# W2 sums on POOL, later low parts and spread stores in a linear-attention and two-MoE kernel

## The chip, the cores and the metric

The kernel runs on one core of one Trainium2 chip. The metric is the device time of one execution in microseconds (us), lower is better. Engines: TensorE (PE, with its weight loads PEld), VectorE (DVE), ScalarE (ACT), GpSimd (POOL) and SyncE (SP), which here only issues DMA transfers. Each engine works through its own list in order; semaphores order the lists among each other.

## The reference

Three stages in float32. Linear attention with a root-mean-square norm gives x of N = 2304 rows and D = 512 columns. A dense mixture of E = 8 experts (F = 1024) follows, whose gates come from 8 Sinkhorn rounds; then a second mixture in which each row goes to one expert, chosen by the cosine to an embedding.

```python
kv = einsum('bhsd,bhse->bhde', k, v); out = einsum('bhsd,bhde->bhse', q, kv)
x = out / sqrt(mean(out * out) + 1e-6) * g_norm
P = exp(x @ w_gate - max)
for _ in range(8):
    P /= P.sum(1, keepdims=True) + 1e-9
    P /= P.sum(0, keepdims=True) + 1e-9
    P *= N / E
x2 = sum over e of P[:, e:e+1] * (maximum(x @ w1[e], 0) @ w2[e])
expert = argmax(cosine(x2, expert_emb) / tau); gate = softmax at expert
out[rows of e] = gate * (maximum(x2 @ w1b[e], 0) @ w2b[e])
```

## The kernel before

**Number format.** Every float32 operand is split in two: a high part (`wh`, made on ScalarE, line 163) and a low part, the difference (`wl`, line 168 on POOL in two halves of 512 columns, line 170 on VectorE in one piece). A product is three matmuls: high x high, high x low, low x high.

**Steps.** The dense mixture is done in 3 blocks of 768 rows. Block b and expert e make step s = 8 b + e, 24 steps. Each has an up phase (7 products `n` = 0 to 6 with W1, a fast matrix scheme that needs sums and differences of the quarters of W1 and x; 4 positions `i` each, 28 positions, 6 matmuls a position) and a down phase with W2. In block 0 (steps 0 to 7) the down phase is plain: 4 parts `m` of 6 positions. In steps 8 to 22 it uses the fast scheme as well (7 products of 3 positions), and so needs differences of the quarters of W2. Step 23 is followed by the second mixture.

In the profiled execution steps 1 to 9 begin their up phases at 151.71, 222.43, 293.39, 357.47, 429.06, 497.20, 566.51, 631.83 and 696.25 us; step 15 at 1052.38, step 16 at 1112.26, step 17 at 1180.34. The fast steps between last about 59.3 us each. The down phases of steps 2 to 7 begin at 256.84, 324.79, 394.67, 462.78, 531.96 and 598.55.

**Weights ahead.** `ahead(g)` (line 936, called in the second position of each up product and the third of each down part) prepares part g + 3 with `prep`: the high part on ScalarE, the low part on POOL for n in 3, 5, 6, 8, 9 and on VectorE else, and for n = 2 and 3 two differences of quarters on POOL (line 255). Four slots (`g % 4`) hold the parts. `keep` stores some parts in DRAM (`w1c`), so that blocks 1 and 2 `fetch` them (line 268) and needn't split again. Raw weights come by `load_quarter` and `load_second` into a ring of six tiles.

**W2 for the fast scheme.** In steps 2 to 7, 32 rounds `r` run between the positions (`thooks`, counted from the first position of step 2; round r starts at position a = 10 + 9 r): `t_load` loads two rows of tiles at a, `t_sums` makes four differences of 128x256 on VectorE at a + 7 and a + 8 (line 1020), `t_high` the high part on ScalarE at a + 11 (line 1024), `t_low` the low part on POOL at a + 12 (line 1029), and `t_store` writes both to DRAM (`w2c`, line 1035) at a + 15 and a + 19.

**Up phase and banks.** Products n = 1, 4, 6 accumulate on the PSUM banks of n = 0, 3, 5. For n = 4, 5, 6 `hidden` adds on VectorE (line 918), applies the ReLU on ScalarE (line 920) and makes the low part on VectorE one position later (line 915); n = 5 and n = 6 share banks, so the addition of n = 5 has to be done before the same position of n = 6, four positions on.

**Other work between positions.** Each position runs a hook of the list `hooks` (steps 0 to 2: the rest of attention, then 8 Sinkhorn rounds of `sk_row` on VectorE, `sk_col`, a small matmul with the column sums `cs`, line 647, and `sk_scale`), then one of `dhooks` (`load_emb`, `dots`: products of the finished rows with the embeddings). When expert 7 has added to a row tile, `finished` stores it to `x2d` on SyncE (line 974) at once, and in blocks 0 and 1 puts its squares on ScalarE off to the third position of a product of the next step.

Of the kernel before, what the change touches and what calls it, by code (L numbers as in the profile page):

```python
# [8 lines left out]
F32 = mybir.dt.float32  # L9
F32R = mybir.dt.float32r  # L10
BF16 = mybir.dt.bfloat16
I32 = mybir.dt.int32
AF = mybir.ActivationFunctionType
ALU = mybir.AluOpType
# [3 lines left out]
N, D, E, F = B * S, H * HD, 8, 1024  # L18
P = 128
# [21 lines left out]
def f32(ap):  # L41
    return ap.bitcast(F32)

@with_exitstack
def tile_linattn_moe_moe(ctx: ExitStack, tc: tile.TileContext, qT, k, v, g2, wg, w1a, w2a, emb, embT, tau, w1b, w2b, out):
    nc = tc.nc
# [114 lines left out]
    def split_into(raw, hi, lo, eng=None, hi_eng=None):  # L161
        if hi_eng is None:
            nc.scalar.copy(hi, raw)  # L163
        else:
            hi_eng.tensor_copy(hi, raw)
        if eng is nc.gpsimd and dense[0]:
            for c in (slice(0, 512), slice(512, 1024)):
                eng.tensor_tensor(lo[:, c], raw[:, c], f32(hi[:, c]), ALU.subtract)  # L168
        else:
            (eng or nc.vector).tensor_tensor(lo, raw, f32(hi), ALU.subtract)  # L170
        return hi, lo
# [10 lines left out]
    W2ORDER = (2, 3, 0, 1)  # L182
    CACHED = {2: 0, 3: 1, 5: 2, 6: 3}
    DOWN = (("b", 0, 0), ("b", 1, 0), ("t", 3), ("t", 1), ("t", 0), ("t", 2), ("b", 1, 1))
    NSTEP = NBK * E
    raws = {}
    parts = {}
# [17 lines left out]
    def slot_tiles(g):  # L205
        return (wp.tile([P, 1024], F32R, tag=f"g{g % 4}h", name="wh", bufs=1),
                wp.tile([P, 1024], F32R, tag=f"g{g % 4}l", name="wl", bufs=1))

    def load_quarter(s, name, t=None):
        t = t if t is not None else raw_tile()  # L210
        r, c = {"w11": (0, 0), "w12": (1, 0), "w21": (0, 1), "w22": (1, 1)}[name]
        nc.sync.dma_start(
            t.rearrange("p (k f) -> p k f", k=2), w1a[s % E, :, 2 * r:2 * r + 2, c * 512:(c + 1) * 512])
        raws[s, name] = t

    def spare(s, name):
        raws[s, name] = raw_tile()
# [5 lines left out]
    def load_second(s, q):  # L223
        raws[s, q] = load_w2(lambda j: w2a[s % E, :, 2 * j:2 * j + 2, :].rearrange("p a d -> p (a d)"), js=(q,))[0]

    def load_plain(g):
# [7 lines left out]
                              w2a[s % E, :, 4 * a:4 * a + 4, c * 256:(c + 1) * 256])  # L234
        raws[g] = t

    def prep(g, lo_eng=None):
        s, n = seq_of[g]

        def r(name):  # L240
            return raws[s, name]

        if g in plain_at:
            src = raws[g]
        elif n >= 7:
            src = r(W2ORDER[n - 7])
        else:
            if n == 2 and s == 0:
                sums(s)
            src = r(("w11", "w12", "s2", "w21", "w22", "s1", "w12")[n])  # L250
        parts[g] = split_into(src, *slot_tiles(g), lo_eng)
        if s < E and n in (2, 3):
            o, a, b = (r(i) for i in (("w21", "w11", "w21"), ("w12", "w12", "s2"))[n - 2])
            for c in (slice(0, 512), slice(512, 1024)):
                nc.gpsimd.tensor_tensor(o[:, c], a[:, c], b[:, c], ALU.subtract)
# [56 lines left out]
    xj = rt.tile([P, 2 * D], F32, name="xj")  # L312
    x2t, junk = xj[:, 0:D], xj[:, D:2 * D]
# [3 lines left out]

    late = ExitStack()
    axp = late.enter_context(tc.tile_pool(name="ax", bufs=1, side="right"))
    ax = [axp.tile([P, D], F32, name=f"ax{i}") for i in range(6)]  # L320
    qxa = axp.tile([P, 3 * D], F32, name="qxa")
    qx = [qxa[:, i * D:(i + 1) * D].rearrange("p (k n) -> p k n", k=KC) for i in range(3)]
    kvbd = [qx[2]] + [ax[i].rearrange("p (k n) -> p k n", k=KC) for i in range(3)]
# [165 lines left out]
    for c in range(NSC):  # L489
        n = rows_of(c)  # L490
# [40 lines left out]
    x2d = dp.tile([N + P, D], F32, name="x2d")  # L531
# [7 lines left out]
    rb = up.tile([P, 2, D], F32, name="rb")  # L539
# [65 lines left out]
    hooks = []  # L605
# [56 lines left out]
    ssq = rt.tile([P, NT], F32, name="ssq")  # L662
# [35 lines left out]
    def load_emb(e):  # L698
        nc.sync.dma_start(qx[e % 3].rearrange("p k n -> p (k n)"), emb[e:e + 1, :].to_broadcast([P, D]))
# [86 lines left out]
    def seq(*fs):  # L786
        return lambda: [g() for g in fs]
# [148 lines left out]
    def ahead(g):  # L936
        h = g + 3
        if h < len(seq_of):
            s, n = seq_of[h]
            if s < E or h in plain_at or n >= 7 and not quick(s):  # L940
                pool = n in POOL_LOW and (s, n) != (NSTEP - 1, 9) if s < E or not quick(s) and n >= 7 else True
                prep(h, nc.gpsimd if pool else None)
            else:
                fetch(h)
            keep(h - 1)
        for h in plain_load.get(g, ()):
            load_plain(h)
        s, n = seq_of[g]
        if (s < E or s == NSTEP - 1) and n < 3:
            for q in (W2ORDER[0:2], W2ORDER[2:3], W2ORDER[3:4])[n]:  # L950
                load_second(s, q)
        if s + 1 < E:
            if n == 3:
                load_quarter(s + 1, "w11")
                load_quarter(s + 1, "w21")
            elif n == 4:
                load_quarter(s + 1, "w22")
            elif n == 5:
                spare(s + 1, "s1")
            elif n == 6:  # L960
                spare(s + 1, "s2")
            elif n == 7:
                load_quarter(s + 1, "w12")
        elif s == NSTEP - 1 and n > 2:
            for f in {3: [lambda: early_w1(0), lambda: early_w1(1)], 4: [lambda: early_w1(2)], 5: [lambda: early_w1(3)],
                      6: [lambda: early_w2(0)], 7: [lambda: early_w2(1)]}.get(n, ()):
                f()

    squared = []

    def finished(t):
        a = acc_of(t)
        r = t if t < T1 else t + 1
        nc.sync.dma_start(x2d[r * P:(r + 1) * P, :], a)
        square = lambda: nc.scalar.activation(junk, a, AF.Square, accum_out=ssq[:, t:t + 1])
        if t // JT + 1 < NBK:
            squared.append(square)
        else:
            square()

    def add(t, e, ps):
        a = acc_of(t)
# [15 lines left out]
    tick = [0]  # L998

    def run_thooks():  # L1000
        if s >= 2:
            for f in thooks.pop(tick[0], ()):
                f()
            tick[0] += 1

    rhs = [[qxa[:, 0:512], qxa[:, 512:1024]], [qxa[:, 1024:1536], pBw[:, 0:512]]]

    def t_bufs(r):
        two = [[rb[:, 0, :], rb[:, 1, :]], [x2t, junk]]
        return two[r] if r < 2 else [ax[0:2], ax[2:4], two[0], two[1], ax[4:6]][(r - 2) % 5]  # L1010

    def t_load(r):
        e, f = divmod(r, 4)
        for a in range(2):
            nc.sync.dma_start(t_bufs(r)[a], w2a[e, :, f + 4 * a, :])

    def t_sums(r, i):
        b11, b12, b21, b22 = (t[:, c * 256:(c + 1) * 256] for t in t_bufs(r) for c in range(2))
        for o, x, y in ((b11, b12, b11), (b12, b12, b22), (b22, b22, b11), (b21, b21, b22))[2 * i:2 * i + 2]:
            nc.vector.tensor_tensor(o, x, y, ALU.subtract)  # L1020

    def t_high(r):
        for a in range(2):
            nc.scalar.copy(rhs[r % 2][a].bitcast(F32R), t_bufs(r)[a])

    def t_low(r):
        for a in range(2):
            t = t_bufs(r)[a]
            nc.gpsimd.tensor_tensor(t.bitcast(F32R), t, rhs[r % 2][a], ALU.subtract)

    def t_store(r, i):
        e, f = divmod(r, 4)
        for a in range(2):
            t = t_bufs(r)[a] if i else rhs[r % 2][a]
            nc.sync.dma_start(
                w2c[e, 2 * a:2 * a + 2, i, :, f, :].rearrange("w p c -> p w c"),
                t.rearrange("p (w c) -> p w c", w=2))
# [100 lines left out]
    for i in range(m + 3):  # L1138
        o = (lambda i=i: stream_out(*sg[i])) if i < m else rest
        r = (lambda i=i: stream_root(*sg[i])) if i < m else rest  # L1140
# [6 lines left out]
    hooks[-1] = idle_rows  # L1147
    hooks.extend([sk_max, rest, rest, sk_max1, rest, rest, sk_exp, rest, rest])
    for i in range(8):
        hooks.extend([sk_row, rest, rest, sk_col, rest, sk_scale] + [rest] * (i < 7))  # L1150
    n_hooks = len(hooks)
    dhooks = []
    xq = []

    for s in range(NBK * E):
        blk, e = divmod(s, E)
        final = s == NBK * E - 1
        if e == 0 and blk > 0:
            dhooks.extend([seq(lambda: load_emb(0), lambda: load_emb(1), lambda: load_emb(2))] + [rest] * 12)
            for ee in range(E):  # L1160
                for t in range((blk - 1) * JT, blk * JT):
                    dhooks.append(lambda t=t, ee=ee: dots(t, ee))
                    if t % 2:
                        dhooks.append(rest)
                if ee + 3 < E:
                    dhooks.append(lambda ee=ee: load_emb(ee + 3))
# [13 lines left out]
        if s == 2:  # L1180
            for r in range(4 * E):
                a = 10 + 9 * r
                for at_, f in ((a, t_load), (a + 7, lambda r: t_sums(r, 0)), (a + 8, lambda r: t_sums(r, 1)),
                               (a + 11, t_high), (a + 12, t_low),
                               (a + 15, lambda r: t_store(r, 0)), (a + 19, lambda r: t_store(r, 1))):
                    thooks.setdefault(at_, []).append(lambda f=f, r=r: f(r))
        fast = quick(s)
        if final:
# [556 lines left out]
```

## Time and profile before

| | |
|---|---|
| three timed runs | 1896.48, 1903.59 (median), 1905.62 us |
| profiled execution, its own time | 1906.41 us |
| its span, first to last instruction | 1904.2 us |
| mean granted TensorE clock | 0.985 |
| TensorE busy | 1825.6 us (96%) |
| VectorE busy | 1329.3 us (70%) |
| POOL busy | 912.2 us (48%) |
| ScalarE busy | 845.2 us (44%) |
| DMA moved | 397.75 MB, mean 209 GB/s |

An engine's busy share is a mean over the whole span; who bounds a phase is read from waits and from windows of that phase. In an instruction's group, `wl<-raw,wh` names the tile written and the tiles read. In a list of waits the instruction on the left sat idle until the one on the right was done.

### The profile page before, as it was taken

To read this page: it belongs to the slowest core of one execution; us is meant where nothing else is said; L and a number is where in the kernel's file an instruction comes from. 1 tells how busy PE (TensorE), PEld (TensorE's weight loads), DVE (VectorE), ACT (ScalarE), POOL (GpSimd) and SP (SyncE) were. 2 spreads that over 40 slices of the span, in tenths; PEclk is the share of its full clock that TensorE was granted. 3 is DMA by queue.
4 is the path that set the end of the run, shared out by engine and by line. 5 is a ranking of instruction groups with operands and counts; after the bars stand their busy time and mean duration, and the time that the engine had idled before them with its cause. 6 is when DMAs were issued, how large, how long until landed. Compare 5 with 4: busy or idle time off the path is not lost. (4 is left out here: it accounts for less than half of the span.)

```text
span 1904.2 us, 31099 instructions
## 1 busy us (share of the span) xinstructions
PE 1825.6 (96%) x11494; PEld 1723.4 (91%) x11494; DVE 1329.3 (70%) x2389; ACT 845.2 (44%) x1437; POOL 912.2 (48%) x713
## 2 busy tenths in 40 slices
PE   7899999999999999999999989999999999899997
PEld 7889878878888899999999989999999998778996
DVE  4865588678678588964556668986567763877665
ACT  3545334334334534544355445454454433345443
POOL 1412245546546466654466457745466432544111
PEclk9999999999999999999999999999999999899999
DMA  9625267767768665564655755565555653378664
GB/s 290 213 62 194 92 218 276 252 239 257 261 229 299 222 218 205 186 229 168 211 189 180 263 183 201 197 228 183 194 190 189 220 192 119 139 278 280 231 223 157
DMA packets 185570, 397.75 MB, mean 209 GB/s; under 512 B 16448, under 2 KB 86592, under 8 KB 185408
## 3 DMA queue, kind: packets, MB, share of 16 engines
q1 hardware_dynamic: 179680, 378.33, 58.1%
q0 software_dynamic: 4000, 13.11, 2.1%
q10 hardware_dynamic: 1728, 4.23, 0.6%
q8 instruction: 92, 1.51, 0.3%
q14 instruction: 70, 0.57, 0.1%
HBM read 314.61 MB, written 81.00 MB: 208 GB/s over the span
## 5 line engine op out<-in xcount | busy, mean ns | idle before, releaser
L930 PE MATMUL A<-xo,wh 128*128 128x384 f32 x2688 | 696.8, 340 | 25.8 <-DVE dl L915 7.2
L930 PEld LDWEIGHTS A<-xo,wh 128*128 128x128 f32 x2688 | 487.9, 190 | 35.7 <-DVE dl L915 9.5
L930 PE MATMUL A<-xo,wl 128*128 128x384 f32 x1344 | 454.2, 338 | 2.5 <-DMA wl<-w1c 2.5
L168 POOL TENSOR_TENSOR wl<-raw,wh 128x512 fp32r<-128x512 f32 x180 | 256.3, 1446 | 371.6 <-ACT wh L163 178.5
L1063 PE MATMUL A<-wh,dl 128*128 128x256 f32 x1260 | 356.6, 283 | 0.3 <-POOL dl L1117 0.3
L1063 PE MATMUL A<-wh,dh 128*128 128x256 f32 x1260 | 356.8, 283 | 0.0
L1063 PE MATMUL A<-wl,dh 128*128 128x256 f32 x1260 | 356.5, 283 | 0.0
L930 PEld LDWEIGHTS A<-xo,wl 128*128 128x128 f32 x1344 | 255.6, 190 | 3.4 <-DMA wl<-w1c 3.4
L1063 PEld LDWEIGHTS A<-wh,dl 128*128 128x128 f32 x1260 | 241.8, 192 | 0.5 <-POOL dl L1117 0.5
L1063 PEld LDWEIGHTS A<-wl,dh 128*128 128x128 f32 x1260 | 241.7, 192 | 0.0
L1063 PEld LDWEIGHTS A<-wh,dh 128*128 128x128 f32 x1260 | 241.7, 192 | 0.0
L915 DVE SCALAR_TENSOR_TENSOR dl<-A,dh 128x384 fp32r<-128x384 f32 x228 | 125.3, 552 | 146.8 <-ACT raw L1210 93.1
L168 POOL TENSOR_TENSOR wl<-rb,wh 128x512 fp32r<-128x512 f32 x92 | 129.8, 1431 | 176.0 <-ACT wh L163 175.7
L163 ACT CAST wh<-raw 128x1024 fp32r<-128x1024 f32 x139 | 145.5, 1047 | 72.6 <-PE A L1272 40.0
L920 ACT ACTIVATE dh<-A 128x384 fp32r<-128x384 f32 x132 | 65.4, 496 | 246.4 <-DVE A L918 246.2
L1272 PE MATMUL A<-wh,dh 128*128 128x512 f32 x384 | 153.2, 399 | 5.0 <-DVE dl L915 4.9
L1272 PE MATMUL A<-wl,dh 128*128 128x512 f32 x384 | 150.6, 392 | 0.0
L1272 PE MATMUL A<-wh,dl 128*128 128x512 f32 x384 | 150.5, 392 | 0.0
L1206 ACT COPY qs<-A 128x384 f32<-128x384 f32 x96 | 46.1, 481 | 192.7 <-PE A L930 192.1
L170 DVE TENSOR_TENSOR wl<-raw,wh 128x1024 fp32r<-128x1024 f32 x49 | 74.2, 1515 | 42.5 <-ACT wh L163 31.3
L1272 PEld LDWEIGHTS A<-wh,dh 128*128 128x128 f32 x384 | 72.7, 189 | 21.7 <-DVE dl L915 7.1
L1113 POOL TENSOR_TENSOR dl<-qs,dh 128x384 fp32r<-128x384 f32 x60 | 64.0, 1100 | 50.0 <-ACT dh L1111 50.0
(490 smaller groups left out, 3579.5 us busy)
## 6 DMA issues: line engine op xcount, KB each, us to landing
raw<-in_w1a_dram SPq DMA_DIRECT2D x64, 512.0 KB, 4.6
wh<-w1c SPq DMA_DIRECT2D x64, 512.0 KB, 5.4
wl<-w1c SPq DMA_DIRECT2D x64, 512.0 KB, 6.2
wh<-w2c SPq DMA_DIRECT2D x60, 512.0 KB, 5.1
wl<-w2c SPq DMA_DIRECT2D x60, 512.0 KB, 5.8
raw<-in_w2a_dram SPq DMA_DIRECT2D x51, 512.0 KB, 4.4
raw<-in_w1b_dram SPq DMA_DIRECT2D x48, 512.0 KB, 5.8
raw<-in_w2b_dram SPq DMA_DIRECT2D x48, 512.0 KB, 3.9
```

Source lines behind the costliest of these rows:

```text
L163: nc.scalar.copy(hi, raw)
L168: eng.tensor_tensor(lo[:, c], raw[:, c], f32(hi[:, c]), ALU.subtract)
L170: (eng or nc.vector).tensor_tensor(lo, raw, f32(hi), ALU.subtract)
L915: nc.vector.scalar_tensor_tensor(hl[:, i, :], src, 0.0, f32(hh[:, i, :]), ALU.max, ALU.subtract)
L920: nc.scalar.activation(hq[a][0][:, i, :], dst, AF.Relu)
L930: nc.tensor.matmul(ps[:, 0:HB], a[:, fs], bb[:, kk, :], start=(first and j == 0), stop=(j == 5), skip_group_check=True)
L1063: nc.tensor.matmul(o, a[:, f, ts_], bb[:, ds_], start=(m in first and j != 1 and i == 0), stop=(i == 11), skip_group_check=True)
L1113: nc.gpsimd.tensor_tensor(a12[1][:, i], qs[:, i], f32(a12[0][:, i]), ALU.subtract)
L1206: nc.scalar.copy(qs[:, i, :], p)
L1272: nc.tensor.matmul(ys[j], a, bb[:, ds_], start=(m + ff + i == 0), stop=(m == 3 and ff == 1 and i == 2))
```

## The change

Low parts on VectorE (block 0, from part 3 on): `prep` makes only the high part and puts the low part in a list `after_two`, with a count of 2 that is lowered at the end of each position, the present one included, so that it is issued at the end of the position after it, behind that position's own VectorE work. Loads that `ahead` issues queue behind it when the list isn't empty. The W2 sums are three POOL operations: one of 128x512 with a broadcast operand, two of 128x256; the tiles `ax` become slices of one tile for that. The rounds' offsets move: sums at a + 9, high at a + 14, low at a + 15, stores at a + 18 and a + 22. `finished` puts off the row store with the squares, so one store goes out in each product n = 1 to 6 of the next step. The three first embedding loads move from one hook at the head of the list to three hooks after four rests, and 10 rests follow in place of 12. In a Sinkhorn round `sk_col` comes five positions behind `sk_row` (before: three), `sk_scale` one behind that, and each round takes seven hooks.

```diff
+    after_two = []
+
+    def run_after():
+        for t in after_two:
+            t[0] -= 1
+        while after_two and after_two[0][0] <= 0:
+            after_two.pop(0)[1]()
...
-        parts[g] = split_into(src, *slot_tiles(g), lo_eng)
+        hi, lo = parts[g] = slot_tiles(g)
+        if s < E and lo_eng is None and g > 2:
+            nc.scalar.copy(hi, src)
+            after_two.append([2, lambda: nc.vector.tensor_tensor(lo, src, f32(hi), ALU.subtract)])
+        else:
+            split_into(src, hi, lo, lo_eng)
...
-    ax = [axp.tile([P, D], F32, name=f"ax{i}") for i in range(6)]
+    axa = axp.tile([P, 6 * D], F32, name="ax")
+    ax = [axa[:, i * D:(i + 1) * D] for i in range(6)]
...
+        for f in loads:
+            if after_two:
+                after_two.append([2, f])
+            else:
+                f()
...
-        nc.sync.dma_start(x2d[r * P:(r + 1) * P, :], a)
-        square = lambda: nc.scalar.activation(junk, a, AF.Square, accum_out=ssq[:, t:t + 1])
+
+        def store():
+            nc.sync.dma_start(x2d[r * P:(r + 1) * P, :], a)
+            nc.scalar.activation(junk, a, AF.Square, accum_out=ssq[:, t:t + 1])
+
         if t // JT + 1 < NBK:
-            squared.append(square)
+            squared.append(store)
...
     def run_thooks():
+        run_after()
...
-    def t_sums(r, i):
-        b11, b12, b21, b22 = (t[:, c * 256:(c + 1) * 256] for t in t_bufs(r) for c in range(2))
-        for o, x, y in ((b11, b12, b11), (b12, b12, b22), (b22, b22, b11), (b21, b21, b22))[2 * i:2 * i + 2]:
-            nc.vector.tensor_tensor(o, x, y, ALU.subtract)
+    def t_sums(r):
+        b = t_buf(r).rearrange("p (a d) -> p a d", a=4)
+        nc.gpsimd.tensor_tensor(
+            b[:, 0:2], b[:, 1:2].to_broadcast([P, 2, 256]), b[:, 0:4:3], ALU.subtract)
+        nc.gpsimd.tensor_tensor(b[:, 3], b[:, 3], b[:, 0], ALU.subtract)
+        nc.gpsimd.tensor_tensor(b[:, 2], b[:, 2], b[:, 3], ALU.subtract)
...
-        hooks.extend([sk_row, rest, rest, sk_col, rest, sk_scale] + [rest] * (i < 7))
+        hooks.extend([sk_row, rest, rest, rest, rest, sk_col, sk_scale])
...
-            dhooks.extend([seq(lambda: load_emb(0), lambda: load_emb(1), lambda: load_emb(2))] + [rest] * 12)
+            dhooks.extend([rest] * 4 + [lambda i=i: load_emb(i) for i in range(3)] + [rest] * 10)
...
-                for at_, f in ((a, t_load), (a + 7, lambda r: t_sums(r, 0)), (a + 8, lambda r: t_sums(r, 1)),
-                               (a + 11, t_high), (a + 12, t_low),
-                               (a + 15, lambda r: t_store(r, 0)), (a + 19, lambda r: t_store(r, 1))):
+                for at_, f in ((a, t_load), (a + 9, t_sums), (a + 14, t_high), (a + 15, t_low),
+                               (a + 18, lambda r: t_store(r, 0)), (a + 22, lambda r: t_store(r, 1))):
```

## Rows read from the trace of the kernel before

**Rows 1.** The page's summary: busy us (share of the span) and instructions.

```profile
...
PE 1825.6 (96%) x11494; PEld 1723.4 (91%) x11494; DVE 1329.3 (70%) x2389; ACT 845.2 (44%) x1437; POOL 912.2 (48%) x713
...
```

**Rows 2.** TensorE's waits, whole run: line <- releaser: us in total, times, longest.

```profile
...
PE A L930 <- DVE dl L915: 7.2, 5, 2.4
...
PE A L930 <- DVE u L1215: 5.7, 5, 2.3
PE A L930 <- DMA wh<-w1c: 5.5, 2, 3.2
PE M L647 <- DVE cs L642: 5.4, 3, 2.6
PE A L930 <- DVE u L918: 5.3, 8, 2.6
PE A L1272 <- DVE dl L915: 4.9, 4, 2.0
...
PE A L930 <- DMA wl<-w1c: 2.5, 3, 1.3
...
```

**Rows 3.** Windows: us, busy by engine (instructions), granted clock, DMA share, GB/s.

```profile
...
324.79:357.47 32.68, 32.68 (x145) 27.03 (x145) 24.48 (x32) 10.59 (x16) 20.04 (x13) 1.00 0.70 237
...
sum 409.40, PE 385.42 PEld 341.45 DVE 315.94 ACT 165.57 POOL 228.20; mean PE 32.12 PEld 28.45 DVE 26.33 ACT 13.80 POOL 19.02
...
sum 205.87, PE 200.91 PEld 164.38 DVE 158.28 ACT 68.69 POOL 117.58; mean PE 33.49 PEld 27.40 DVE 26.38 ACT 11.45 POOL 19.60
...
631.83:666.03 34.20, 31.25 (x170) 30.63 (x168) 17.91 (x36) 18.31 (x42) 10.14 (x9) 0.95 0.67 239
696.25:725.38 29.13, 29.13 (x170) 29.13 (x169) 23.19 (x54) 15.68 (x32) 10.37 (x8) 1.00 0.66 223
1112.26:1150.12 37.86, 32.80 (x171) 31.76 (x170) 18.80 (x39) 18.84 (x43) 16.15 (x15) 0.91 0.70 245
...
```

**Rows 4.** VectorE instructions, steps 2 to 7: count, duration ns min/median/max, form.

```profile
...
L1020 DVE TENSOR_TENSOR ax<-ax x36: 414/426/1535, 271.7 to 613.7; 128x256 f32<-128x256 f32 x36
...
L170 DVE TENSOR_TENSOR wl<-raw,wh x33: 1186/1227/2325, 232.5 to 606.5; 128x1024 fp32r<-128x1024 f32 x33
...
L915 DVE SCALAR_TENSOR_TENSOR dl<-A,dh x72: 541/547/559, 228.6 to 605.3; 128x384 fp32r<-128x384 f32 x72
...
```

**Rows 5.** VectorE's waits, steps 2 to 7.

```profile
...
DVE wl L170 <- ACT wh L163: 17.8, 11, 5.3
...
DVE ax L1020 <- DMA ax<-in_w2a_dram: 8.2, 5, 3.6
...
```

**Rows 6.** POOL, steps 2 to 7: durations ns min/median/max; then count | busy us, mean ns.

```profile
...
L168 POOL TENSOR_TENSOR wl<-raw,wh x62: 1286/1312/2157, 226.5 to 615.2; 128x512 fp32r<-128x512 f32 x62
...
L255 POOL TENSOR_TENSOR raw<-raw 128x512 f32<-128x512 f32 x22 | 34.7, 1597 | 10.1 <-issue 7.8 <-DVE raw L220 2.4
...
L282 POOL TENSOR_TENSOR xo<-u,xo 128x384 fp32r<-128x384 f32 x4 | 4.0, 1010 | 0.0
...
```

**Rows 7.** ScalarE's waits, steps 2 to 7.

```profile
...
ACT qxa L1024 <- DVE ax L1020: 25.9, 9, 7.7
...
```

**Rows 8.** Window of one lowered clock.

```profile
...
184.70:188.10 3.40, 3.40 (x12) 3.40 (x11) 3.40 (x7) 1.25 (x3) 1.65 (x2) 0.50 0.00 0
...
```

**Rows 9.** VectorE's waits, steps 0 and 1.

```profile
...
DVE wl L170 <- ACT wh L163: 11.7, 7, 5.0
...
```

**Rows 10.** Timeline of TensorE at 184 and at 647: start, us, what, idle before.

```profile
...
183.97 0.39 PE L647 MATMUL M<-cs,ones 128*128 128x8 f32 x2 [1.81 <-DVE cs L642]
...
646.86 0.59 PE L930 MATMUL A<-xo,wh 128*128 128x384 f32 x2 [2.35 <-DMA wh<-w1c]
...
```

**Rows 11.** Timeline of SyncE's DMA issues at steps 8 and 16.

```profile
...
634.06 3.59 SPq L699 DMA_DIRECT2D qxa<-in_emb_dram  x3
638.07 0.33 SPq L268 DMA_DIRECT2D wh<-w1c  x1
...
1122.44 0.33 SPq L268 DMA_DIRECT2D wh<-w1c  x1
...
```

More of the change, by code (lines that the diff above doesn't have):

```diff
@@ L948, in ahead @@
         s, n = seq_of[g]
+        loads = []
         if (s < E or s == NSTEP - 1) and n < 3:
[L950 to L964, printed above, removed]
+            loads = [lambda q=q: load_second(s, q) for q in (W2ORDER[0:2], W2ORDER[2:3], W2ORDER[3:4])[n]]
+        if s + 1 < E and n in (3, 4, 7):
+            loads = [lambda w=w: load_quarter(s + 1, w) for w in {3: ("w11", "w21"), 4: ("w22",), 7: ("w12",)}[n]]
+        elif s + 1 < E and n in (5, 6):
+            spare(s + 1, "s1" if n == 5 else "s2")
+        for f in loads:
[3 more added lines that the diff above has]
+                f()
+        if s == NSTEP - 1 and n > 2:
             for f in {3: [lambda: early_w1(0), lambda: early_w1(1)], 4: [lambda: early_w1(2)], 5: [lambda: early_w1(3)],
@@ L973, in finished @@
         r = t if t < T1 else t + 1
-        nc.sync.dma_start(x2d[r * P:(r + 1) * P, :], a)
-        square = lambda: nc.scalar.activation(junk, a, AF.Square, accum_out=ssq[:, t:t + 1])
+        def store():
+            nc.sync.dma_start(x2d[r * P:(r + 1) * P, :], a)
+            nc.scalar.activation(junk, a, AF.Square, accum_out=ssq[:, t:t + 1])
         if t // JT + 1 < NBK:
-            squared.append(square)
+            squared.append(store)
         else:
-            square()
+            store()
     def add(t, e, ps):
@@ L1006, in tile_linattn_moe_moe, with t_buf @@
     rhs = [[qxa[:, 0:512], qxa[:, 512:1024]], [qxa[:, 1024:1536], pBw[:, 0:512]]]
-    def t_bufs(r):
-        two = [[rb[:, 0, :], rb[:, 1, :]], [x2t, junk]]
-        return two[r] if r < 2 else [ax[0:2], ax[2:4], two[0], two[1], ax[4:6]][(r - 2) % 5]
+    def t_buf(r):
+        two = [rb.rearrange("p a d -> p (a d)"), xj]
+        return two[r] if r < 2 else [axa[:, 0:1024], axa[:, 1024:2048], two[0], two[1], axa[:, 2048:3072]][(r - 2) % 5]
     def t_load(r):
@@ L1014, in t_load @@
         for a in range(2):
-            nc.sync.dma_start(t_bufs(r)[a], w2a[e, :, f + 4 * a, :])
-    def t_sums(r, i):
-        b11, b12, b21, b22 = (t[:, c * 256:(c + 1) * 256] for t in t_bufs(r) for c in range(2))
-        for o, x, y in ((b11, b12, b11), (b12, b12, b22), (b22, b22, b11), (b21, b21, b22))[2 * i:2 * i + 2]:
-            nc.vector.tensor_tensor(o, x, y, ALU.subtract)
+            nc.sync.dma_start(t_buf(r)[:, a * D:(a + 1) * D], w2a[e, :, f + 4 * a, :])
+    def t_sums(r):
[4 more added lines that the diff above has]
+        nc.gpsimd.tensor_tensor(b[:, 2], b[:, 2], b[:, 3], ALU.subtract)
     def t_high(r):
         for a in range(2):
-            nc.scalar.copy(rhs[r % 2][a].bitcast(F32R), t_bufs(r)[a])
+            nc.scalar.copy(rhs[r % 2][a].bitcast(F32R), t_buf(r)[:, a * D:(a + 1) * D])
     def t_low(r):
         for a in range(2):
-            t = t_bufs(r)[a]
+            t = t_buf(r)[:, a * D:(a + 1) * D]
             nc.gpsimd.tensor_tensor(t.bitcast(F32R), t, rhs[r % 2][a], ALU.subtract)
@@ L1033, in t_store @@
         for a in range(2):
-            t = t_bufs(r)[a] if i else rhs[r % 2][a]
+            t = t_buf(r)[:, a * D:(a + 1) * D] if i else rhs[r % 2][a]
             nc.sync.dma_start(
```

## Prediction

> **What bounds the kernel now.** I read the engine summary first: TensorE is busy for 96% of the span and every other engine for 70% or less [rows 1]. So a change to VectorE, POOL or SyncE pays only where TensorE now waits for one of them, and at most by those waits and by what the lowered clock after a wait costs. The table of TensorE's waits says who it waits for [rows 2]: VectorE's results in the up products (dl, u: 7.2 + 5.7 + 5.3 us), the same at the start of the down products (4.9, 23.1 together), the Sinkhorn column sums cs (5.4), and transfers of cached weights (5.5 + 2.5).
>
> Then I place them by windows of single phases. An up phase with nothing in its way (the one from 696.25) is 29.13 us and a down phase of block 0 (from 324.79) is 32.68 us [rows 3], so a clear step of block 0 is 61.8 us and steps 2 to 7 would be 370.9. They take 409.4 (the sum of twelve windows) [rows 3]: 38.5 us over, of which about 2 are the extra small products of the Sinkhorn steps, so some 36 can be won there. The up phases that open steps 8 and 16 take 34.20 and 37.86 us: 5.1 and 8.7 over, with a mean granted clock of 0.95 and 0.91.
>
> **POOL takes the W2 sums.** Removed: 4 subtractions on VectorE for each of 32 rounds, all in steps 2 to 7. The median one is 0.426 us and the longest 1.535 [rows 4], so 128 of them hold VectorE for 54 us at the least, and VectorE idled 8.2 us more before those on one tile alone for their loads [rows 5]. Why some are three times as long: the 1024-wide low part on VectorE, which reads two SBUF tiles, takes 1.186 to 2.325 us, while the low part that reads PSUM takes 541 to 559 ns in all of 72 cases [rows 4]. Only the SBUF readers stretch, and by about the length of one POOL subtraction. The Trainium skill says so in "SBUF — State Buffer", Who interferes with whom: a VectorE instruction with two SBUF inputs and a GpSimd instruction that reads SBUF exclude each other for a whole instruction. The trace agrees (0.426 against 1.535 us), and by that rule the sums move from one side of the lock to the other and don't leave it.
>
> Added on POOL: one 128x512 and two 128x256 subtractions a round. The 512-wide kind takes 1.29 us at best, 1.31 in the median, and 1.60 in the mean of the slowest group; 128x384 takes 1.010 [rows 6]. No 256-wide one is in the trace: it lies between VectorE's 0.43 [rows 4] and the 512-wide 1.29, and the line through 1.010 and 1.29 gives 0.73, which I take. A round is 1.29 + 2 x 0.73 = 2.75 us, 88 us for 32; with the bounds 69 to 124. In a clear up phase of 28 positions (1.04 us each), 3.1 rounds fall: 8.6 us. POOL is busy 228.2 us in the six steps and 117.6 of these in their down phases (the two sums) [rows 3], so 18.4 per up phase; with 8.6 it is 27.0 of 29.13. Per down phase it is 19.6 + 2.67 x 2.75 = 26.9 of 32.68. POOL fits, and only just.
>
> In the Trainium skill, "GPSIMD Engine Reference", section 3 (Performance versus the Vector engine) speaks against the move: an elementwise operation with two inputs costs there about twice VectorE's time. By that figure the sums would be an estimated 128 x 0.426 x 1.96 = 107 us on POOL, inside the bounds above.
>
> Who waits for POOL: ScalarE's high part stands 5 positions (5.2 us) behind the sums. They take 2.8, so a POOL queue of over 2.4 us holds ScalarE, in order, with the ReLUs behind it. Ahead of a round's sums in an up phase can stand a low-part pair (2.6 us), a difference pair (2.6) and the round before's low pair (2.6), so ScalarE will be held for 0 to 5 us about twice in an up phase. That is not new: it waits for VectorE's sums today, 25.9 us on one tile alone [rows 7]. TensorE feels it when VectorE's additions, which take turns with low parts that wait for a ReLU, are three positions (3.1 us) late, since the next product accumulates into the same bank. I put 1 to 2 us for each of six up phases, and half clock after about half of these (3.4 us at 0.5, the lower of the two levels, 1.2 for 2.4 GHz, costs 1.7 [rows 8]): 12 us. The low parts that still meet POOL's lock (33 of 1024 columns, 24 of 384) I charge with another 4. So of the 36 us, 16 stay: **gain 20**; ends: 36, and a loss of 30 (first rival).
>
> **Low parts two positions later.** VectorE stood still for 17.8 us in steps 2 to 7 before 11 of these because ScalarE's high part was not there [rows 5]. That is part of what makes it late, and is in the 20. A part is used 11 positions after it is queued, so two positions cost nothing. The stores of cached parts are issued four or more positions behind, after the low part. The weight loads queued behind a deferred low part go out 1 to 2 us later on SyncE, which takes nothing from the five phases or more before their use. In steps 0 and 1 VectorE lost 11.7 us before 7 of them [rows 9]; TensorE's longest wait for u, 2.3 us [rows 2], is in step 0, and I credit 1 (ends 0 and 4, that wait and its clock).
>
> **Sinkhorn spacing.** The column product waits for cs: 1.81 us at 184 [rows 10], with half clock after it, and twice in step 2 (counted above). It comes two positions later, 2.1 us, than the row sums; where VectorE is no later, step 1's 1.81 + 1.7 us go. I take 3 (ends 0 and 3.5). The added position makes the chain one hook longer; it still ends in step 2.
>
> **Row stores and embedding loads.** At the start of step 8 SyncE issues three row stores, three embedding loads (3.59 us with their waits), and only then, at 638.07, the fetch of the fourth part [rows 11]; TensorE waits for that part until 646.86 [rows 10]. Now that fetch comes behind none of these and can go at about 633.5, in the first product's second position, when TensorE has left the slot. It landed 8.8 us after issue, and would by 642.3; it is needed twelve positions into the step, at 631.83 + 12.5 = 644.3. In step 16 the same: fetch at 1122.44 behind stores and loads [rows 11], and of the waits for cached parts 5.1 us are there (8.0 in all [rows 2], less 2.4 + 0.6 at step 8). What is late next there: SyncE stands, ahead of the third part's fetch, for a plain load that waits for POOL's low part, and the third part lands close to its need eight positions in, at 1112.26 + 8.3 = 1120.6. The excess is 5.1 + 8.7 = 13.8; stores of 0.25 MB, one per phase, go beside fetches that now have no TensorE wait in the other fast steps. **Gain 11**; ends 0 and 13.8, or a loss of 4 (one wait of the size of today's and its clock) if spread stores delay a later part. The products with the embeddings start four hooks later; 94 hooks in four steps of 31 positions hold them.
>
> **Sum.** The profiled execution took 1906.41 us, 2.8 above the median of the three timed runs, which lie between 1896.48 and 1905.62. 1906.4 - 20 - 11 - 3 - 1 = 1871.4; from the median the same saving gives 1868.6. I forecast 1870.
>
> **Rivals.** (a) POOL becomes the bound in steps 2 to 7, slower than before. The six steps hold 64 halves of low parts, 64 of the rounds' and 22 of differences, 25 512-wide operations a step, and 5.33 rounds of 1 + 2 x 0.57 = 2.14 such, 36.4 in all, so POOL fills a clear step of 61.8 us when the mean reaches 1.70 us. One of its groups is at 1.60 now [rows 6], and the waits for ScalarE's casts come on top. From there each late low part stops TensorE and takes its clock. At 5 us more per step than today, or 73 per step, the six steps cost +30: 1906 + 30 - 15 = 1921. For it: the up phases are full by my own sum. Against: 128 fewer VectorE operations contend for the lock, so the mean should fall and not rise. 0.12.
> (b) POOL's lateness returns what VectorE gives: steps 2 to 7 stay near 68 us, and only the other parts remain: 1906.4 - 15 = 1891. 0.18.
> (c) All of VectorE's waits go, POOL's queue never reaches TensorE: 36 + 13 + 3.5 + 2.5 = 55 us, 1851. For it: step 3's down phase already runs clear with these sums on VectorE [rows 3]; it asks that no ScalarE hold lasts over 3 us. 0.13.
> (d) The spread transfers only move the waits at steps 8 and 16 to later parts: 1871 + 11 = 1882. For it: the DMA engines are 0.67 to 0.70 busy there [rows 3]. 0.10.
> (e) The spacing changes don't reach the waits (VectorE late for another reason), all parts worth a few us: within 1897 to 1912. 0.07. The forecast keeps 0.40.
>
> **How the numbers follow.** A difference under 0.5% (9.5 us) can't be told from none. The forecast, (c) and (d) are faster throughout (0.63), (b) mostly (0.15 of 0.18), (a) slower (0.11 of 0.12), (e) in the middle: faster 0.79, same 0.10, slower 0.11. The likeliest case's own range is 1860 to 1882. The range 1853 to 1900 leaves out (a), most of (e) and the far half of (c).
>
> **What would show it.** Right: no subtraction of the W2 sums on VectorE, its busy time in steps 2 to 7 some 60 us or more lower, POOL's some 80 to 100 us higher; steps of about 65 us; PE waits for dl and u down from some 23 to under 10 us in the table; no wait for transfers of cached parts at 640 to 650 and none over 1 us in step 16's first phases; no wait for cs before 200. Wrong: PE waits named POOL (low parts), ScalarE waiting for POOL's sums for over 5 us at a time, the mean of POOL's 512-wide subtractions above 1.6 us, or steps 8 and 16 still above 62 us.

## The result and the profile after

The changed kernel takes 1854.88 us in the median (1852.14 to 1860.29), the one before 1903.51: ratio 0.9749, 95% interval 0.9726 to 0.9772, or 48.6 us less. The profiled execution took 1852.14 us (span 1850.4).

The table of TensorE's waits, against [rows 2]. What is left of VectorE's in the up products:

```profile
...
PE A L944 <- DVE u L932: 3.8, 6, 1.6
PE A L944 <- DVE u L1231: 3.5, 2, 2.3
...
PE A L944 <- DVE dl L929: 1.1, 1, 1.1
...
```

VectorE's results cost TensorE 8.4 us instead of 23.1, and 2.3 + 1.1 of that lie in step 0, as before. The waits for the column sums and for cached parts, 5.4 and 8.0 us, are gone from the table, and so are the waits at the start of the down phases.

Steps 2 to 7, step 1, and the up phases of steps 8 and 16 as windows, against [rows 3] (us, busy by engine, granted clock, DMA share, GB/s):

```profile
...
216.83:597.47 380.64, 375.42 (x1889) 338.57 (x1888) 249.03 (x344) 166.60 (x265) 327.10 (x249) 1.00 0.78 265
149.78:216.83 67.05, 67.05 (x357) 60.90 (x355) 42.58 (x89) 27.01 (x44) 19.62 (x15) 1.00 0.45 151
597.47:626.62 29.15, 29.15 (x170) 29.14 (x168) 16.67 (x32) 18.30 (x42) 13.36 (x12) 1.00 0.89 307
1072.85:1101.97 29.12, 29.12 (x170) 29.12 (x169) 17.17 (x35) 18.80 (x43) 16.18 (x15) 1.00 0.84 305
...
```

VectorE's busy time in the six steps fell by 66.9 us (315.9 to 249.0) and POOL's rose by 98.9 (228.2 to 327.1): the work costs more where it now runs, and TensorE still gained 28.8 us there. The clock is at its upper level in all four windows. POOL is busy for 86% of the six steps.

Where the time went, phase by phase (the starts of the phases subtracted, profiled executions):

```
                     before     after    difference
before step 0         51.55     51.13        -0.4
step 0               100.16     98.65        -1.5
step 1                70.72     67.05        -3.7
steps 2 to 7         409.40    380.64       -28.8
step 8, up            34.20     29.15        -5.1
step 16, up           37.86     29.12        -8.7
all others to 23     907.73    907.32        -0.4
after step 23        292.58    287.32        -5.3
```

The stretch behind step 23 has the same code in all kernels here, and takes between 287 and 294 us in the profiled executions: the changed kernel and two of the experiments below (low_only and after_no_low) have the short one. Those 5.3 us are not the change's. Nor is step 0 shown to be: it varies by 1 to 3 us among kernels that are the same there. The change is in 28.8 + 13.8 + 3.7 = 46.3 us; the medians lie 48.6 apart, and the rest is not assigned.

### The profile page after: what moved, and what is told of

It reads as the page before. It is cut to its first block, busy times and chain, and to the rows that moved or that the text cites. A ratio compares the mean times of both kernels' runs of the same rounds, so it can differ in the third digit from the quotient of the medians.

```text
span 1850.4 us, 31040 instructions
## 1 busy us (share of the span) xinstructions
PE 1802.6 (97%) x11494; PEld 1710.4 (92%) x11494; DVE 1256.7 (68%) x2261; ACT 845.5 (46%) x1437; POOL 1015.7 (55%) x809
## 5 line engine op out<-in xcount | busy, mean ns | idle before, releaser
L944 PE MATMUL A<-xo,wh 128*128 128x384 f32 x2688 | 686.8, 336 | 9.8 <-DVE u L932 3.8
L944 PEld LDWEIGHTS A<-xo,wh 128*128 128x128 f32 x2688 | 482.2, 188 | 14.6 <-DVE u L932 3.8
L944 PE MATMUL A<-xo,wl 128*128 128x384 f32 x1344 | 449.5, 334 | 0.0
L1080 PEld LDWEIGHTS A<-wh,dh 128*128 128x128 f32 x1260 | 241.8, 192 | 0.0
L163 ACT CAST wh<-raw 128x1024 fp32r<-128x1024 f32 x94 | 98.2, 1047 | 10.5 <-issue 2.8
L1499 POOL DMA_INDIRECT out_dram<-y,idx x18 | 19.0, 1058 | 138.2 <-DVE y L1498 133.2
L262 DVE TENSOR_TENSOR wl<-raw,wh 128x1024 fp32r<-128x1024 f32 x45 | 69.7, 1551 | 27.5 <-ACT wh L261 19.0
```

Of the source, the lines that this page charges most:

```text
L262: after_two.append([2, lambda: nc.vector.tensor_tensor(lo, src, f32(hi), ALU.subtract)])
L944: nc.tensor.matmul(ps[:, 0:HB], a[:, fs], bb[:, kk, :], start=(first and j == 0), stop=(j == 5), skip_group_check=True)
L1080: nc.tensor.matmul(o, a[:, f, ts_], bb[:, ds_], start=(m in first and j != 1 and i == 0), stop=(i == 11), skip_group_check=True)
```

## The experiments

All are compared by their phases, each from one profiled execution; medians of the whole stand beside them. Steps 9 to 15 agree to 0.1 us in all kernels, and so does step 1 in those that are the same there. Steps 2 to 7 are less steady: spread_only, which touches them only at their end, differs there by 0.6 us from the kernel before, and step 4 of after_no_spacing moved by 1.5 us with nothing changed in it. So differences of that size can't be given to a cause there without a wait that names it.

**One part alone: stores and embedding loads spread.**

```diff
 (before)
-        nc.sync.dma_start(x2d[r * P:(r + 1) * P, :], a)
-        square = lambda: nc.scalar.activation(junk, a, AF.Square, accum_out=ssq[:, t:t + 1])
+
+        def store():
+            nc.sync.dma_start(x2d[r * P:(r + 1) * P, :], a)
+            nc.scalar.activation(junk, a, AF.Square, accum_out=ssq[:, t:t + 1])
+
         if t // JT + 1 < NBK:
-            squared.append(square)
+            squared.append(store)
...
-            dhooks.extend([seq(lambda: load_emb(0), lambda: load_emb(1), lambda: load_emb(2))] + [rest] * 12)
+            dhooks.extend([rest] * 4 + [lambda i=i: load_emb(i) for i in range(3)] + [rest] * 10)
```

> The kernel before with only the row stores and the three first embedding loads spread. Theory A (SyncE's queue was what the cached parts waited for): the up phases of steps 8 and 16 fall from 34.20 and 37.86 us to 29.1 to 29.2, steps 2 to 7 stay at 409 +- 3, time some 13.8 us lower, about 1890. Rival B (those waits come from POOL and VectorE being late at the end of the block, and go only with their relief): at least one of the two phases stays above 32 us and the time falls by less than 8.

1889.09 us, ratio 0.992 (0.9895 to 0.9946). Steps 2 to 7, then the up phases of steps 8 and 16:

```profile
...
220.49:629.30 408.81, 385.05 (x1890) 341.30 (x1888) 316.90 (x473) 165.56 (x265) 227.85 (x156) 0.99 0.73 251
...
629.30:658.45 29.15, 29.15 (x170) 29.15 (x169) 16.66 (x32) 18.31 (x42) 9.99 (x9) 1.00 0.74 249
1104.66:1133.79 29.13, 29.13 (x170) 29.13 (x169) 17.19 (x35) 18.84 (x43) 16.18 (x15) 1.00 0.83 298
...
```

Theory A: both phases are clear, and steps 2 to 7 stayed within 0.6 us.

**One part alone: the sums on POOL** (with the new offsets; the other parts undone).

> The kernel before with only the sums of W2 as three POOL operations at the new offsets; low parts, stores, loads and Sinkhorn spacing as before. Theory A (VectorE's occupied time is what TensorE waited for in steps 2 to 7): these steps fall from 409.4 to 385 to 392 us, time 18 to 24 us lower, 1880 to 1886. Rival B (VectorE's standing before low parts, in its queue's order, is the larger cause): 398 to 404 us, time 6 to 11 us lower.

1881.21 us, ratio 0.9884 (0.9857 to 0.9911). Steps 2 to 7, then the same two up phases:

```profile
...
220.97:604.24 383.27, 376.22 (x1890) 338.23 (x1889) 253.90 (x345) 166.44 (x265) 327.04 (x249) 1.00 0.78 264
...
604.24:639.88 35.64, 32.34 (x169) 31.54 (x168) 17.90 (x36) 18.29 (x42) 13.32 (x12) 0.90 0.74 255
1086.10:1124.26 38.16, 32.88 (x170) 31.77 (x169) 18.63 (x39) 18.82 (x43) 16.16 (x15) 0.91 0.71 247
...
```

26.1 us of the 28.8 come by this part alone, more than theory A's 17 to 24. The two up phases get no shorter, even 1.4 and 0.3 us longer, so the spreading is needed for those.

**One part alone: the low parts later** (sums as four VectorE operations at the old offsets).

> The kernel before with only the low parts of VectorE two positions later (and the loads behind them); sums as four VectorE operations at the old offsets. Theory A: VectorE still holds the sums' 85 us, so steps 2 to 7 fall by 4 to 10 us only, and step 1 by under 2. Rival B: they fall by 15 us or more.

1897.86 us, ratio 0.9964 (0.9948 to 0.9981). Steps 2 to 7, step 1, then the up phase of step 8:

```profile
...
219.52:625.05 405.53, 383.07 (x1890) 339.84 (x1888) 320.66 (x472) 165.33 (x265) 228.72 (x156) 0.99 0.73 252
150.70:219.52 68.82, 67.54 (x357) 60.77 (x355) 43.20 (x89) 27.04 (x44) 19.54 (x15) 1.00 0.43 147
625.05:655.96 30.91, 29.66 (x169) 29.05 (x168) 17.81 (x36) 18.30 (x42) 9.94 (x9) 1.00 0.76 263
...
```

3.9 us off steps 2 to 7, a little under theory A's 4 to 10, and 1.9 off step 1. VectorE's wait for ScalarE's high part before its low parts fell from 17.8 us [rows 5] to 5.5 in steps 2 to 7:

```profile
...
DVE wl L262 <- ACT wh L261: 5.5, 5, 1.4
...
```

So 12 us less of standing made the steps only 3.9 us shorter: the standing was not the larger part of what made VectorE late. What no forecast had: the up phase that opens step 8 (the third window) is 30.91 us here and not 34.20, with stores and embedding loads at their old place, while step 16's stayed at 37.92. So some 3.3 of the 5.1 us at step 8 can be had by either part; why is open.

**All but the engine: the sums back on VectorE.**

```diff
 (after, t_sums)
-        nc.gpsimd.tensor_tensor(
-            b[:, 0:2], b[:, 1:2].to_broadcast([P, 2, 256]), b[:, 0:4:3], ALU.subtract)
-        nc.gpsimd.tensor_tensor(b[:, 3], b[:, 3], b[:, 0], ALU.subtract)
-        nc.gpsimd.tensor_tensor(b[:, 2], b[:, 2], b[:, 3], ALU.subtract)
+        ve = nc.vector
+        ve.tensor_tensor(b[:, 0], b[:, 1], b[:, 0], ALU.subtract)
+        ve.tensor_tensor(b[:, 1], b[:, 1], b[:, 3], ALU.subtract)
+        ve.tensor_tensor(b[:, 3], b[:, 3], b[:, 0], ALU.subtract)
+        ve.tensor_tensor(b[:, 2], b[:, 2], b[:, 3], ALU.subtract)
```

> The changed kernel with the four sums back on VectorE at the new offset (a + 9), all else as changed. Theory A (the engine counts): steps 2 to 7 rise from 380.6 to 395 to 402 us, time 15 to 21 us above the changed kernel. Rival B (the later offsets and low parts were enough): they rise by less than 8 us. In both the lowered clocks tell: by A two or more come back between 217 and 600 us.

1882.75 us, ratio 0.989 (0.9864 to 0.9916):

```profile
...
216.97:625.42 408.45, 384.80 (x1890) 344.00 (x1888) 327.66 (x472) 165.51 (x265) 223.01 (x155) 0.98 0.72 249
...
```

27.8 of the 28.8 us are lost again, more than theory A had said, and four lowered clocks come back between 247 and 580 us. The engine is the cause. All other parts together leave 1.0 us here, less than the 3.9 of the low parts alone. The four sums stand in one position in this run and in two positions in low_only; what took the other 3 us is not shown.

**Leaving one part out: the low parts, and the Sinkhorn spacing.**

```diff
 (after_no_low)
-        if s < E and lo_eng is None and g > 2:
+        if False and s < E and lo_eng is None and g > 2:
 (after_no_spacing)
-        hooks.extend([sk_row, rest, rest, rest, rest, sk_col, sk_scale])
+        hooks.extend([sk_row, rest, rest, sk_col, rest, sk_scale] + [rest] * (i < 7))
```

> The changed kernel with VectorE's low parts back at their old place, everything else as changed. If the parts simply add, as the single ones did (the low parts alone took 3.9 us off steps 2 to 7 and 1.9 off step 1), steps 2 to 7 rise from 380.6 to 383 to 385 and step 1 from 67.05 to 68.9: time 4 to 7 us above the changed kernel. Rival: with the sums on POOL ScalarE runs later, so that an early low part holds VectorE for longer and costs more than alone: steps 2 to 7 above 388.

> The changed kernel with the Sinkhorn hooks spaced as before (the column product three positions behind the row sums). Theory A (the spacing takes away the wait for the column sums): step 1 rises from 67.05 to 68.8 us, as in the kernel with the low parts alone, and TensorE's waits name the column sums again, some 1 to 2.5 us. Rival B (with VectorE relieved the column sums are in time anyway): step 1 stays within 0.3 us of 67.05. For step 2, where the kernel without deferred low parts was 1.4 us longer than one with the old spacing too: by A its up phase stays at 32.3 +- 0.5; if the new spacing costs something there, it falls to 31.5 or below.

1861.74 us (ratio to before 0.9782, 0.9766 to 0.9799) and 1862.77 us (0.9792, 0.977 to 0.9814). Steps 2 to 7 and step 1, first without the later low parts:

```profile
...
221.07:605.72 384.65, 378.03 (x1890) 339.89 (x1888) 255.34 (x348) 166.68 (x265) 325.93 (x249) 1.00 0.76 262
152.50:221.07 68.57, 67.45 (x356) 60.84 (x355) 39.10 (x86) 26.99 (x44) 19.64 (x15) 1.00 0.43 147
...
```

and with the old spacing:

```profile
...
219.90:603.50 383.60, 377.62 (x1889) 339.64 (x1888) 248.85 (x344) 166.07 (x265) 326.32 (x249) 1.00 0.76 263
151.12:219.90 68.78, 67.54 (x356) 60.80 (x355) 43.16 (x89) 27.02 (x44) 19.51 (x15) 1.00 0.42 147
...
```

In the changed kernel the low parts are worth 4.0 us in steps 2 to 7 and 1.5 in step 1, about as much as alone. But the parts don't simply add. With the old spacing the later low parts gain nothing in steps 2 to 7 beside the sums on POOL (383.27 us in pool_only, 383.60 in after_no_spacing), and without the later low parts the new spacing gains nothing there either (384.65 in after_no_low). Only with both are these steps at 380.64.

Without the spacing TensorE waits 3.8 us for the column sums, 1.2 in step 1 and 2.6 in step 2, more than the 1 to 2.5 expected, and step 1 is 1.7 us longer: theory A. Steps 2 to 7 are 3.0 us longer, of which 1.4 in step 2's up phase, where the last rounds run, and 1.5 in step 4, where no round runs: that much of it is not the rounds' own. For step 2 both forecasts failed: its up phase neither stayed at 32.3 us nor fell, but rose to 33.7. (Where the low parts are not deferred it is the other way: step 2's up phase is 35.01 us in after_no_low and 33.63 in pool_only, with the old spacing. Why is open.)

**How much ScalarE's holds cost.** Three kernels move the rounds' high and low parts.

```diff
 (after: offsets of t_sums, t_high, t_low, stores)
-  a + 9, a + 14, a + 15, a + 18, a + 22
+  a + 9, a + 11, a + 12, a + 18, a + 22      # after_high11
+  a + 9, a + 17, a + 18, a + 21, a + 25      # after_high17
+  a + 9, a + 17, a + 18, a + 21, a + 24      # high17_store24
```

> The changed kernel with ScalarE's high parts of the rounds at a + 11 and POOL's low parts at a + 12, as far behind the sums as before the change, in place of a + 14 and a + 15. ScalarE's waits for POOL's sums (59.5 us in steps 2 to 7 of the changed kernel) grow to 110 to 160 us. Theory A (TensorE pays for what a hold exceeds three positions): steps 2 to 7 rise from 380.6 by 8 to 20 us. Rival B (what is left of TensorE's waits comes from VectorE at POOL's lock and not from ScalarE): they rise by less than 3 us.

> The changed kernel with the high parts at a + 17, the low parts at a + 18 and the stores at a + 21 and a + 25. ScalarE's waits for POOL's sums fall below 25 us. Theory A: steps 2 to 7 fall from 380.6 to 375 to 378 us. Rival B: they stay at 379 to 382 us.

> The changed kernel with the high parts at a + 17, the low parts at a + 18, the stores at a + 21 and a + 24, the last store before its buffer is loaded again. From the run with a + 25: steps 2 to 7 at 378 +- 1 us against 380.6, ScalarE held for POOL's sums by some 28 us, no lowered clock in these steps. Time 1852 to 1856; a gain of 2 us over the changed kernel is below what the total can tell. If the earlier store holds SyncE, the phases show it: any of steps 3 to 7 longer than in the run with a + 25 by over 0.5 us.

In after_high17 the last low parts in the buffer `rb` are stored (584.1 us) after its next load was issued (576.9), so W2's low parts are wrong there; its times are readable. High11 is harder than its text says: its high parts stand two positions behind the sums, and before the change they stood three behind the second pair of sums. Medians 1877.71, 1855.35 and 1855.16 us (ratios to before 0.986, 0.9736 and 0.9743). Steps 2 to 7 of the first and the last:

```profile
...
215.85:616.01 400.16, 382.94 (x1889) 343.28 (x1888) 249.00 (x344) 166.02 (x265) 320.01 (x250) 0.98 0.74 255
...
```

```profile
...
214.83:592.72 377.89, 374.31 (x1889) 338.61 (x1888) 248.47 (x344) 165.44 (x265) 325.20 (x247) 1.00 0.77 268
...
```

With high11, ScalarE is held for 96 us and not for the 110 to 160 expected, and steps 2 to 7 are 19.5 us longer: theory A, at the upper end of its 8 to 20. The two high17 kernels gain 2.4 and 2.8 us of the phases, with 28 and 38 us of holds left, not under 25: 378.3 us lies between the two forecasts, 377.9 just inside theory A's. Nearly all of it is the up phase of step 4, which is clear now (the changed kernel, then high17_store24):

```profile
...
345.57:377.17 31.60, 29.73 (x170) 29.09 (x169) 18.65 (x32) 16.30 (x28) 27.48 (x22) 1.00 0.82 278
...
```

```profile
...
343.28:372.43 29.15, 29.15 (x169) 29.14 (x168) 19.53 (x34) 16.66 (x29) 25.02 (x20) 1.00 0.84 283
...
```

No phase of steps 3 to 7 is longer with the store at a + 24 than at a + 25. In the total the gain does not show: high17_store24 is the version that the phases point to, and its median equals the changed kernel's within what can be told.

**How much POOL can still take.**

```diff
 (after, behind t_sums; n = 2 and 4)
+        for _ in range(n):
+            nc.gpsimd.tensor_tensor(pBw[:, 512:768], b[:, 0], b[:, 1], ALU.subtract)
```

> The changed kernel with two more 128x256 POOL subtractions behind each round's sums, into unused columns: 64 of some 0.9 us, 58 us more on POOL, which is then 385 us in steps of 381. Theory A (POOL becomes the bound where its work fills the step): steps 2 to 7 rise to 388 to 405 us. Rival B (POOL's idle time is not usable, because its list waits for casts, so it is the bound well before it is full): above 410 us. Rival C (a late POOL only delays what has slack): under 385 us.

> The same with four more 128x256 subtractions a round, 115 us more, 442 us of POOL's work. Theory A: steps 2 to 7 rise to 435 to 455 us, POOL busy over 95% of them, and TensorE's waits name POOL's low parts. Rival B: above 460 us. Rival C: under 420 us.

1883.49 us (ratio 0.9877, 0.9842 to 0.9912) and 1931.94 us (1.0141, 1.011 to 1.0172). Steps 2 to 7 with two more and with four more:

```profile
...
221.34:623.19 401.85, 382.90 (x1889) 343.08 (x1888) 258.13 (x343) 165.88 (x265) 374.67 (x310) 0.98 0.73 250
...
```

```profile
...
220.41:667.73 447.32, 398.10 (x1889) 353.99 (x1888) 249.65 (x341) 163.70 (x263) 417.61 (x372) 0.94 0.66 224
...
```

TensorE's waits in steps 2 to 7 with four more:

```profile
...
PE A L944 <- ACT qs L1224: 14.4, 6, 3.6
PE A L944 <- DVE u L932: 11.8, 5, 3.7
PE A L944 <- POOL wl L168: 11.6, 10, 4.1
...
```

Theory A in both sizes. The first 47.6 us more of POOL's busy time lengthen the steps by 21.2, the next 42.9 by 45.5, and POOL is 93% busy in both (374.7 of 401.9, 417.6 of 447.3): there its work sets the time, at 93% and not at the 95% I had named. VectorE is not behind it, whose busy time is 9 us higher with two more and about unchanged with four. The first to tell of it are ScalarE and VectorE, who wait for POOL; POOL's own name comes third. A single phase can be fuller without harm. In the changed kernel POOL is busy for 98% of step 5's down phase, and that phase is clear:

```profile
...
439.95:472.63 32.68, 32.68 (x146) 27.04 (x145) 18.38 (x20) 10.34 (x15) 32.05 (x25) 1.00 0.87 300
...
```

## Why the prediction was right, and where its size was off

**Which rival it is.** The direction, the mechanism and the range held, the range by only 2 us: its lower end was 1853. The forecast was 1870; 1854.9 stands beside the 1851 of rival (c), to which I gave 0.13. Of rival (c) only the size came: VectorE's waits did not all go, and 7.7 us of excess are left. Two of the signs that I had named for being wrong are in the trace all the same: ScalarE stands for POOL's sums for 5.3 us at a time (below), and the mean of POOL's 512-wide W2 sums is 1.67 us, above my 1.6. Over all of POOL's 512-wide subtractions in these steps the mean is 1.50, against 1.52 before. So both signs tell of a queue on POOL, which is there, and not of what it costs.

**Steps 2 to 7: the mis-sized term.** I left 16 us of the 36 with TensorE: 12 for ScalarE's holds with half clock after them, 4 for POOL's lock. Measured: 380.64 - 370.9 = 9.7 us over a clear run, 2 of them the extra products that I had set aside, so 7.7 stay and the gain is 28.8 and not 20. The holds themselves are there: ScalarE's waits for POOL's sums in the changed kernel, the largest of nine lines that add up to 59.5 us, against 34.8 for VectorE's sums before (its largest line: [rows 7]):

```profile
...
ACT qxa L1041 <- POOL ax L1034: 16.4, 7, 5.3
ACT qxa L1041 <- POOL xj L1034: 11.3, 4, 3.7
...
```

What was wrong is their price. One place where the chain went as I had written it, in step 4, the longest wait of TensorE in these steps: ScalarE first, then VectorE, then TensorE (start, us, what, idle before):

```profile
...
370.64 0.62 ACT L1041 CAST qxa<-ax 128x512 fp32r<-128x512 f32 x1 [1.44 <-POOL ax L1034]
372.28 0.62 ACT L1041 CAST pB<-ax 128x512 fp32r<-128x512 f32 x1 [1.01 <-POOL ax L1037]
...
```

```profile
...
373.35 0.56 DVE L929 SCALAR_TENSOR_TENSOR dl<-u,dh 128x384 fp32r<-128x384 f32 x1 [2.82 <-ACT dh L934]
...
```

```profile
...
374.43 0.62 PE L944 MATMUL A<-xo,wh 128*128 128x384 f32 x2 [1.64 <-DVE u L932]
...
```

ScalarE is held for 1.44 and 1.01 us, VectorE stands 2.82 us for the ReLU behind, and TensorE 1.64 us for VectorE's next addition. I had charged each up phase with that and a lowered clock every second time; the up phases of steps 5 and 6 had none (29.15 and 29.14 us), the clock fell in none of the six, and the waits left in these steps add up to 5.0 us. Ordered by ScalarE's holds (the waits of line 1041 or 1043 for POOL's sums, added up) the experiments show no price per hold:

```
                 ScalarE held by POOL's sums    steps 2 to 7
high17_store24           37.7 us                  377.9
after                    59.5                     380.6
after_high11             96.4                     400.2
pool_plus2              127                       401.9
pool_plus4              169                       447.3
```

Up to 60 us of holds stand beside an excess of 10 at most; 37 more, in after_high11, cost 19.5, and the next 31, in pool_plus2, only 1.7. The five kernels differ in more than the holds, so this is no curve; what it shows is that the sum of the holds doesn't set the price. Before the change 34.8 us of holds stood beside an excess of 38.5 us: ScalarE's holds were not the cause then, VectorE's own occupied time was (pool_only and after_vector_sums). With 67 us of that gone nearly all holds are absorbed. That it is the slack in positions that absorbs them fits the two sides of the experiment, three positions less for the high parts (+19.5 us) and three more (-2.8), and is not shown more directly. I had read the up phases' POOL load (27.0 of 29.13) as a queue at each round. POOL was busy for 25.0 to 27.7 us in the up phases of steps 3 to 7 and for 28.9 to 32.1 in their down phases, where I had 26.9: part of the queue ran on into the down phases.

**POOL's costs.** The 256-wide subtraction takes 0.74 us where I took 0.73, and the 512-wide sum with a broadcast operand 1.30 (durations min/median/max, and counts):

```profile
...
L1036 POOL TENSOR_TENSOR ax<-ax x18: 734/742/1602, 269.4 to 587.8; 128x256 f32<-128x256 f32 x18
...
L1034 POOL TENSOR_TENSOR ax<-ax x18: 1279/1296/2352, 267.0 to 586.4; 128x512 f32<-128x512 f32 x18
...
```

POOL grew by 98.9 us against my 88, inside 69 to 124, but that is two misses that offset each other. The three operations of the rounds alone took 112.7 us (lines 1034, 1036 and 1037):

```profile
...
216.83:597.47 380.64, 53.45 (x32) 1.00 0.78 265
...
```

```profile
...
216.83:597.47 380.64, 29.50 (x32) 1.00 0.78 265
...
```

```profile
...
216.83:597.47 380.64, 29.71 (x32) 1.00 0.78 265
...
```

At the medians above they would be 89; the other 24 us are operations that stretched, as the maxima of 1.60 and 2.35 show, and I had left that out of the 88. And the rest of POOL's work got 13.8 us shorter, which I hadn't counted: about half of that is the differences of quarters, 34.7 us before [rows 6]:

```profile
...
L268 POOL TENSOR_TENSOR raw<-raw 128x512 f32<-128x512 f32 x22 | 28.0, 1296 | 0.0
...
```

On VectorE the sums had taken 86.4 us, and its busy time fell by 66.9: what it kept got longer by the difference.

**Rival (a)** had the mechanism and the wrong distance. It put the bound at a full step, 36.4 operations of 1.70 us; pool_plus2 has it at 93%, where 58 us of planned extra work on POOL are enough. With pool_plus4 the kernel is slower than before, as (a) said.

**Row stores and embedding loads.** I took 11 of 13.8; all 13.8 came. The fetch of the fourth part in step 8 now goes out ahead of the embedding loads and the first store, 4.1 us into the step instead of 6.2 [rows 11]:

```profile
...
601.61 0.41 SPq L281 DMA_DIRECT2D wh<-w1c  x1
602.07 0.44 SPq L281 DMA_DIRECT2D wl<-w1c  x1
602.57 0.90 SPq L713 DMA_DIRECT2D qxa<-in_emb_dram  x2
603.56 0.51 SPq L987 DMA_DIRECT2D x2d<-acc  x1
...
```

I had said 1.7 us into it: SyncE stood until 599.9 for the last round's store, which waits for POOL's low part, a queue that my step had not walked. The part landed in time all the same. Rival (d) fell: no wait came back later, at DMA shares of 0.89 and 0.84.

**Low parts and Sinkhorn spacing.** I credited the low parts with 1 us in steps 0 and 1 and a share of the 20; they give 1.5 to 1.9 in step 1 and 4 in steps 2 to 7, the latter, beside the sums on POOL, only together with the spacing. VectorE's standing before low parts, 17.8 us, did not go as I had it: it is 18.4 in the changed kernel, and 38.4 where the low parts stay at their old place (after_no_low). The spacing gives 1.7 in step 1 where I took 3, and 1.4 more in step 2, which I had counted there.

## What to carry to other kernels

An engine that TensorE waits for is worth emptying even at a higher price elsewhere: 67 us taken from VectorE and 99 given to POOL won TensorE 26 to 28, because VectorE stood in TensorE's chain and POOL's results had five positions until they were used; with two (after_high11) 19.5 us of it were lost again. Count what the receiving engine has left over the whole stretch: here 86% busy left an excess of 8 us in 381, and at 93% it was the bound. Transfers that nobody waits for belong behind the fetch that somebody does.

## What the runs showed of the hardware that was not expected

The same wait lowers the clock in some executions and not in others. In step 0 TensorE waits 2.25 us for `u`, before the change, after it, and in high17_store24, whose step 0 is the same as the changed kernel's:

```profile
...
81.11 0.61 PE L930 MATMUL A<-xo,wh 128*128 128x384 f32 x2 [2.25 <-DVE u L1215]
...
```

```profile
...
80.55 0.62 PE L944 MATMUL A<-xo,wh 128*128 128x384 f32 x2 [2.25 <-DVE u L1231]
...
```

```profile
...
78.46 0.74 PE L944 MATMUL A<-xo,wh 128*128 128x384 f32 x2 [2.25 <-DVE u L1231]
...
```

Before, the clock is at 0.50 right after; in the changed kernel it is at 1.00 over the next 9.5 us; in high17_store24 it is at 0.50 again:

```profile
...
82.30:85.60 3.30, 3.30 (x15) 3.30 (x14) 2.92 (x10) 0.38 (x2) 0.00 (x0) 0.50 0.98 303
...
```

```profile
...
80.50:90.00 9.50, 9.32 (x62) 9.01 (x63) 8.59 (x21) 4.36 (x11) 0.67 (x1) 1.00 0.94 308
...
```

```profile
...
78.80:82.20 3.40, 3.40 (x15) 3.40 (x14) 3.20 (x12) 0.21 (x1) 0.28 (x1) 0.50 0.95 303
...
```

All thirteen profiled executions have this wait, of 2.25 or 2.26 us, and in ten of them the clock fell within 1.6 us behind it; it did not in the changed kernel, after_no_spacing and pool_plus4. So it is not the change that kept the clock up there, and a forecast can't tell for one wait whether the clock will fall. What decides it is open.
